# Refitting a list scheduler's cost model to the trace: engine latencies, transfer time and table loads in a one-core attention-and-MLP kernel

## Chip, core and metric

The kernel runs on one core of a Trainium2 chip. The metric is device time in microseconds (us) of one execution. Medians over several executions are quoted with their range. All runs quoted are in the undisturbed state, at a granted clock of 0.992 or more, except one execution that is named where it occurs. All kernels here give a correct result.

## The reference

`x` is 2048 x 1024, the MLP's inner width is 3584, all in bf16. Cut to what matters:

```python
def reference(A_x, A_wqkv, A_wo, B_x, B_w_gate, B_w_up, B_w_down):
    def _A_ref(x, wqkv, wo):                       # linear attention, 32 heads of 32
        ...                                        # q, k, v = split(x @ wqkv)
        phi = lambda t: jnp.where(t > 0, t + 1, jnp.exp(t)) + 1e-6
        pq, pk = phi(q), phi(k)
        kv = jnp.einsum("bhsd,bhse->bhde", pk, v)
        ...                                        # o = (pq @ kv) / (pq . z)
        return (lambda x, *d: x.transpose(*d))(o, 0, 2, 1, 3).reshape(B, S, D) @ wo
    def _B_ref(x, w_gate, w_up, w_down):
        g = _silu(x @ w_gate)
        u = x @ w_up
        return (g * u) @ w_down
    x = A_x
    xn = _layernorm(x, axis=-1)
    s = _A_ref(xn, A_wqkv, A_wo)
    g = _silu(_B_ref(xn, B_w_gate, B_w_up, B_w_down))
    return x + s * g
```

## The kernel before

The kernel is a program that plans itself on the host. Each piece of work (a group of matmuls, an activation, a VectorE operation, a transfer) becomes an `Op` with an engine, an assumed duration and the data that it reads and writes. `Plan.schedule` plays the program through with these assumed times, and the order in which operations start in that play becomes the order of each engine's queue. `emit` then puts semaphore waits between them. The assumed times never change what is computed. They change above all who stands behind whom in each queue. One thing more hangs on the engine latencies: a load may not be issued before the group of TensorE's work that lies 12 us ahead of its deadline, and the deadlines count these latencies. Run again on the host, the plan after lets 134 of its 257 transfers go later than the plan before, by a median of 1.7 us of TensorE's work; the transfer model, the PE to PE rule and the table part leave these gates where they were.

```python
class Plan:
    ENGS = ("pe", "act", "dve", "pool", "sp")
    LAT = {"pe": 0.25, "act": 0.3, "dve": 0.3, "pool": 0.3}      # from end of work to "others may start"
    ...
    def schedule(self):
        ...                                                       # deadlines o.dl, backwards from TensorE's order
        while len(order) < total:
            best = None
            for e in self.ENGS:
                ...
                if e == "pe":
                    ...                                           # a window of 6 groups
                    rdy = [o for o in cand if o.ready <= t + 0.05]
                    o = min(rdy, key=lambda o: o.idx) if rdy else min(cand, key=lambda o: (o.ready, o.idx))
                else:
                    rdy = [o for o in a if o.ready <= t]
                    o = min(rdy, key=lambda o: (o.dl - o.boost, o.idx)) if rdy else min(a, key=lambda o: (o.ready, o.dl))
                s = max(t, o.ready)
                if best is None or s < best[0]:
                    best = (s, e, o)
            s, e, o = best
            o.start = s
            if o.sem is not None:                                 # a transfer, issued by SyncE
                free[e] = s + 0.08
                b = max(s + 1.0, dma_free)
                dma_free = b + o.nbytes / 230e3
                o.done = dma_free + 1.8
            else:
                free[e] = s + o.busy
                o.done = s + o.busy + o.lat
            ...
            for q in o.succs:
                q.npred -= 1
                q.ready = max(q.ready, o.done)
                if q.npred == 0:
                    avail[q.eng].append(q)
```

The picker for VectorE and ScalarE takes, among the operations that it believes ready, the one with the earliest deadline.

Why TensorE cares about VectorE's order: the large products are done with Strassen-like sets of seven half-size products, and the sums between them are made in PSUM. In a set, ScalarE copies the first product to a second bank, and VectorE adds a stored product to a bank; the next matmuls go on top of that bank.

```python
            def put1(self, a):
                self.a = a
                self.b = balloc()
                act([bank_r[a]], [bank_r[self.b]], ps[self.b][:, :], ps[a][:, :], ACT.Identity)
            ...
                elif m == 6:
                    self.grp(6, self.b, False)
                    self.c = balloc()
                    tt([bank_r[self.b], self.s5.r], [bank_r[self.c]], ps[self.c][:, :], ps[self.b][:, :],
                       self.s5.ap(F32), ALU.add)                  # VectorE: "ps<-ps,TM" in the trace
                ...
                elif m == 3:
                    self.grp(3, self.c, False)                    # TensorE needs that bank
```

The same VectorE queue also takes operations on data that has just been loaded: the layer-norm statistics of each row tile of `x` (`stats<-W`), the sums of weight blocks (`W<-W`, `W<-X`, from `w_gate`, `w_up`, `w_down`), and the last multiply and add of each output tile on transposed data (`TM<-TM`). `x` tiles in the attention part come so:

```python
        def x_load(i):
            s = x_ring.take()
            xslot[i] = s
            dma([], [s.r], s.ap(), xf[i * 128:(i + 1) * 128, :], dsem("x%d" % s.k), 256 * KB).urgent = 10.0

        def ln_tile(i):
            ...
            o0 = dve([s.r], [sA], lambda h: h.bn_stats(stats[:, j, 0, :], xa[:, 0:512]), 512)
            ...
```

## Time and profile before

| kernel before | value |
|---|---|
| median of 3 executions | 731.58 us (731.02 to 731.81) |
| profiled span | 729.5 us |
| TensorE / VectorE / ScalarE busy | 715.9 / 612.8 / 400.5 us |
| table loads on ScalarE | 10, 1.28 us each |

TensorE is busy for 98% of the span, so the reader should look not at shares of busy time but for the few places where TensorE pauses. Two rulers are used. The first is the table of busy time by stretch. The second, finer one is worked out from the trace: the time from one matmul's start to the next, less its columns over 2.4 GHz, counted where more than 40 ns remain. I call these pauses.

One view of the kernel before is not in the prediction, and it turned out to be the one that mattered: the list of what each engine waited for. The columns are engine, what it was about to write, the line of the program, the releaser, then us in total, number of waits and the longest of them.

```profile
DVE W L348 <- DMA W<-in_B_w_down_dram: 7.0, 2, 3.6
DVE TM L348 <- DMA TM<-TM: 3.4, 5, 1.3
DVE stats L649 <- DMA W<-in_A_x_dram: 2.5, 2, 2.4
...
PE ps L210 <- DVE ps L348: 1.4, 5, 0.4
```

Before the change VectorE stood idle ahead of a transfer ten times, 13.2 us in all; TensorE waited for VectorE's additions in PSUM for 1.4 us.

### The profile page before, as it was taken

To read this page: it belongs to the slowest core of one execution; us is meant where nothing else is said; L and a number is where in the kernel's file an instruction comes from. 1 tells how busy PE (TensorE), PEld (TensorE's weight loads), DVE (VectorE), ACT (ScalarE), POOL (GpSimd) and SP (SyncE) were. 2 spreads that over 40 slices of the span, in tenths; PEclk is the share of its full clock that TensorE was granted. 3 is DMA by queue.
4 is the path that set the end of the run, shared out by engine and by line. 5 is a ranking of instruction groups with operands and counts; after the bars stand their busy time and mean duration, and the time that the engine had idled before them with its cause. 6 is when DMAs were issued, how large, how long until landed. Compare 5 with 4: busy or idle time off the path is not lost.

```text
span 729.5 us, 10728 instructions
## 1 busy us (share of the span) xinstructions
PE 715.9 (98%) x3942; PEld 371.1 (51%) x3942; DVE 612.8 (84%) x1443; ACT 400.5 (55%) x759; POOL 14.1 (2%) x35
## 2 busy tenths in 40 slices
PE   8999999999999999999999999999999999999996
PEld 3444444455555555554444445555555555544442
DVE  6999868979989998898555989999999888865662
ACT  3776654787659665654111177676966756511111
POOL 2111000000000000000000000000000000000000
PEclk9999999999999999999999999999999999999999
DMA  8443235135255343324279554134515343546633
GB/s 291 113 104 85 44 107 181 59 107 168 73 159 139 129 143 129 94 73 132 79 186 245 145 165 149 62 116 120 172 59 188 102 130 118 143 123 181 164 89 87
DMA packets 135668, 94.02 MB, mean 129 GB/s; under 512 B 32960, under 2 KB 131520, under 8 KB 135616
## 3 DMA queue, kind: packets, MB, share of 16 engines
q1 hardware_dynamic: 135616, 93.34, 44.9%
q8 instruction: 31, 0.51, 0.3%
q14 instruction: 21, 0.17, 0.1%
HBM read 75.50 MB, written 10.62 MB: 118 GB/s over the span
## 4 chain that ended last, share of the span: by engine, by line
PE 85%; ACT 7%; DVE 5%; issue 2%; POOL 0%; ACTq 0%; DVEq 0%; POOLq 0%
PE ps L210 85%; ACT H L341 3%; ACT TM L341 2%; DVE W L348 2%; DVE H L348 1%; DVE TM L348 1%; ACT ps L341 1%; DVE ps L348 1%; ACT L341 1%; DVE stats L649 0%; DVE stats L653 0%; DVE TM L724 0%; PE ps L217 0%; DVE X L348 0%; POOL rstd L658 0%
## 5 line engine op out<-in xcount | busy, mean ns | idle before, releaser
L210 PE MATMUL ps<-X,W 128*128 128x512 f16 (+1 forms) x1232 | 268.0, 358 | 1.1 <-ACT ps L341 0.5
L341 ACT ACTIVATE TM<-ps 128x512 f16<-128x512 f32 (+2 forms) x345 | 184.2, 553 | 147.8 <-PE ps L210 143.9
L210 PE MATMUL ps<-H,W 128*128 128x512 f16 (+2 forms) x1168 | 256.4, 369 | 0.5 <-DVE ps L348 0.5
L348 DVE TENSOR_TENSOR W<-W 128x256 f16<-128x256 f16 (+5 forms) x440 | 176.4, 437 | 7.2 <-DMA W<-in_B_w_down_dram 7.0
L210 PEld LDWEIGHTS ps<-H,W 128*128 128x128 f16 (+1 forms) x1168 | 113.5, 98 | 124.1 <-DVE ps L348 2.3
L210 PEld LDWEIGHTS ps<-X,W 128*128 128x128 f16 (+1 forms) x1232 | 119.3, 98 | 102.8 <-ACT ps L341 2.2
L348 DVE TENSOR_TENSOR ps<-ps,TM 128x256 f32<-128x256 f32 (+1 forms) x234 | 123.5, 531 | 15.0 <-PE ps L210 14.0
L341 ACT ACTIVATE ps<-ps 128x512 f32<-128x512 f32 (+1 forms) x164 | 81.9, 499 | 72.2 <-PE ps L210 70.1
L210 PE MATMUL ps<-P,W 128*128 128x512 f16 (+1 forms) x496 | 104.7, 329 | 0.7 <-ACT TM L341 0.4
L341 ACT ACTIVATE H<-ps 128x512 f16<-128x512 f32 (+1 forms) x126 | 75.0, 602 | 54.5 <-PE ps L210 54.2
L210 PEld LDWEIGHTS ps<-P,W 128*128 128x128 f16 (+1 forms) x496 | 48.3, 98 | 37.9 <-ACT ps L341 1.0
L348 DVE TENSOR_TENSOR H<-H 128x1024 f16<-128x1024 f16 (+4 forms) x106 | 66.1, 640 | 1.0 <-ACT H L341 0.5
L348 DVE TENSOR_TENSOR TM<-ps,TM 128x512 f32<-128x512 f32 (+1 forms) x60 | 40.7, 678 | 24.0 <-PE ps L210 23.7
L210 PE MATMUL ps<-W 128*128 128x256 f16 (+1 forms) x278 | 56.5, 289 | 0.6 <-DVE ps L348 0.4
L348 DVE TENSOR_TENSOR H<-H,TM 128x512 f16<-128x512 f16 x112 | 44.8, 415 | 14.0 <-ACT H L341 13.8
L341 ACT ACTIVATE TM<-TM 128x512 f16<-128x512 f32 (+1 forms) x61 | 37.9, 624 | 33.4 <-DVE TM L348 32.5
L210 PEld LDWEIGHTS ps<-W 128*128 128x128 f16 (+1 forms) x278 | 26.1, 98 | 21.3 <-DVE ps L348 2.3
L210 PE MATMUL ps<-H,X 128*128 128x512 bf16 (+1 forms) x136 | 32.2, 379 | 1.2 <-ACT X L341 0.8
L210 PE MATMUL ps<-TM,W 128*128 128x256 f16 (+1 forms) x138 | 27.8, 283 | 0.3 <-DVE ps L348 0.3
L348 DVE TENSOR_TENSOR P<-H 128x1024 f16<-128x1024 f16 x28 | 19.0, 686 | 9.2 <-PE ps L210 9.2
L723 DVE TENSOR_SCALAR TM<-TM 128x512 f16<-128x512 f16 x64 | 17.7, 285 | 10.5 <-ACT TM L341 10.3
L348 DVE TENSOR_TENSOR H<-ps,TM 128x512 f16<-128x512 f32 (+1 forms) x35 | 23.9, 682 | 2.3 <-PE ps L210 1.7
(81 smaller groups left out, 394.9 us busy)
## 6 DMA issues: line engine op xcount, KB each, us to landing
W<-in_B_w_down_dram SPq DMA_DIRECT2D x16, 896.0 KB, 5.8
W<-in_B_w_gate_dram SPq DMA_DIRECT2D x12, 1024.0 KB, 5.4
W<-in_B_w_up_dram SPq DMA_DIRECT2D x12, 1024.0 KB, 5.5
W<-in_A_x_dram SPq DMA_DIRECT2D x16, 256.0 KB, 3.0
H<-in_A_wqkv_dram SPq DMA_DIRECT2D x8, 512.0 KB, 8.2
H<-r_scratch SPq DMA_DIRECT2D x32, 128.0 KB, 3.4
W<-m_scratch SPq DMA_DIRECT2D x4, 1024.0 KB, 5.9
s_scratch<-TM SPq DMA_DIRECT2D x32, 128.0 KB, 2.8
```

The lines of the kernel that those rows point to most:

```text
L210: last = h.matmul(o, l, r, start=st, stop=sp, skip_group_check=True)
L341: return PL.op("act", reads, writes, lambda h: h.activation(o, i, func, **kw), nel(o) / 1200.0 + (0.055 if src == "ps" else 0.095))
L348: return dve(reads, writes, lambda h: h.tensor_tensor(o, a, b, op), nel(o), 1.92 if fast else 0.96)
L723: dve([e.r], [b.r], lambda h: h.tensor_scalar(ba, ea, 1.0, EPS_PHI, ALU.min, ALU.add), 512, 2.6)
```

## The change

The intent: make the scheduler's assumed times those which the trace shows, and let it know that ScalarE loads a table when it changes between Exp and Silu. The core of the diff (the `Op` slot, the reset of `tab` and context lines are cut):

```diff
-    LAT = {"pe": 0.25, "act": 0.3, "dve": 0.3, "pool": 0.3}
+    LAT = {"pe": 0.2, "act": 0.165, "dve": 0.14, "pool": 0.15}
...
+                if e == "act" and o.tab is not None and o.tab != tab:
+                    s += TABLE                                   # 1.28
...
+            if o.tab is not None:
+                tab = o.tab
...
-                b = max(s + 1.0, dma_free)
-                dma_free = b + o.nbytes / 230e3
-                o.done = dma_free + 1.8
+                b = max(s + 1.1, dma_free)
+                dma_free = b + o.nbytes / 330e3
+                o.done = dma_free + 1.0
...
-                q.ready = max(q.ready, o.done)
+                q.ready = max(q.ready, o.done if q.eng != "pe" or o.eng != "pe" else s + o.busy)
...
         def act(reads, writes, o, i, func, src="ps", **kw):
-            return PL.op("act", ..., nel(o) / 1200.0 + (0.055 if src == "ps" else 0.095))
+            q = PL.op("act", ..., nel(o) / (1000.0 if "bias" in kw or not isinstance(kw.get("scale", 1.0), float)
+                      else 1200.0) + (0.055 if src == "ps" else 0.095))
+            q.tab = func if func != ACT.Identity else None
+            return q
```

Four parts: engine latencies (LAT), no latency from TensorE to TensorE (PE to PE), the transfer model (DMA), and tables with the slower ScalarE rate.

More of the change, by code (lines that the diff above doesn't have):

```diff
@@ L16 @@
 GRAN = 256
+TABLE = 1.28
 class Op:
     __slots__ = ("eng", "fn", "busy", "lat", "nbytes", "sem", "preds", "succs", "idx", "dl", "start", "done",
-                 "ev", "pecum", "npred", "ready", "urgent", "boost")
+                 "ev", "pecum", "npred", "ready", "urgent", "boost", "tab")
 class Region:
@@ L52, in op @@
         o.boost = 0.0
+        o.tab = None
         o.idx = len(self.ops)
@@ L108, in schedule @@
         dma_free = 0.0
+        tab = None
         avail = {e: [] for e in self.ENGS}
@@ L340, in act @@
         def act(reads, writes, o, i, func, src="ps", **kw):
-            return PL.op("act", reads, writes, lambda h: h.activation(o, i, func, **kw),
-                         nel(o) / 1200.0 + (0.055 if src == "ps" else 0.095))
+            q = PL.op("act", reads, writes, lambda h: h.activation(o, i, func, **kw),
+                      nel(o) / (1000.0 if "bias" in kw or not isinstance(kw.get("scale", 1.0), float) else 1200.0)
+                      + (0.055 if src == "ps" else 0.095))
+            q.tab = func if func != ACT.Identity else None
+            return q
         def dve(reads, writes, fn, n, rate=0.96):
```

## The prediction

> **What bounds the kernel now.** I read the busy line first, then a table of engine busy time by stretch, then TensorE's order of time around each hole in that table.
>
> The engine line and the granted clock, from the page of the kernel before:
>
> ```profile
> PE 715.9 (98%) x3942; PEld 371.1 (51%) x3942; DVE 612.8 (84%) x1443; ACT 400.5 (55%) x759; POOL 14.1 (2%) x35
> PEclk9999999999999999999999999999999999999999
> ```
>
> TensorE is busy 98% of a 729.5 us span at full clock. Only 729.5 - 715.9 = 13.6 us are idle. The change alters no matmul, so it can work only on that idle time and on the short pauses inside "busy". Where are they? Engine busy time by stretch (us from the start; each entry is busy time and number of instructions):
>
> ```profile
> 0.00:8.00 8.00, 6.38 (x22) 2.39 (x22) 3.93 (x11) 1.66 (x2) 4.05 (x21) 1.00 0.61 205
> 8.00:32.00 24.00, 22.24 (x121) 10.13 (x122) 21.79 (x46) 14.18 (x20) 3.42 (x4) 1.00 0.61 196
> 32.00:120.00 88.00, 88.00 (x495) 43.51 (x494) 73.71 (x176) 53.80 (x87) 6.61 (x10) 1.00 0.41 106
> 120.00:140.00 20.00, 18.22 (x105) 9.15 (x103) 19.62 (x63) 13.82 (x26) 0.00 (x0) 1.00 0.35 115
> 220.00:245.00 25.00, 24.17 (x138) 12.77 (x136) 24.24 (x61) 23.59 (x47) 0.00 (x0) 1.00 0.48 130
> 720.00:729.50 9.50, 3.57 (x19) 1.49 (x17) 2.05 (x5) 1.19 (x2) 0.00 (x0) 0.87 0.43 99
> ```
>
> TensorE's column is the third figure. Idle: 1.6 us before 8 us, 1.8 up to 32 us, 1.8 in 120 to 140, 0.8 in 220 to 245, 5.9 after 720; what is left (13.6 - 11.9 = 1.7) lies in 400 to 437 and 465 to 531. All else is full. A stall also hides some 0.16 us in "busy", because a matmul is recorded as 379 ns long while the next can start after 216. So I also summed start-to-start times less columns/2.4 GHz from the trace's matmul starts, counting only excesses over 40 ns. Three heaps come out: 2.7 us in the 14 cold matmuls at the head; 3.3 us of waits between 7.6 and 31.8 us; 8.3 us between 117 and 568 us (2.5 at 134 to 139, 1.6 at 229 to 244, 1.6 at 416 to 436, 1.0 at 466 to 491, 1.0 at 518 to 530, the rest 0.1 or less each). After the last of the big groups comes the tail.
>
> The largest hole, in order of time on ScalarE and TensorE:
>
> ```profile
> 134.78 1.57 ACT L341 ACTIVATE TM<-ps 128x512 f16<-128x512 f32 x3
> 136.37 1.28 ACT L341 ACT_TABLE_LOAD   x1
> 137.66 0.60 ACT L341 ACTIVATE TM<-ps 128x512 f16<-128x512 f32 x1
> 138.31 0.88 PE L210 MATMUL ps<-H 128*128 128x512 bf16 x3 [1.27 <-ACT TM L341]
> ```
>
> TensorE waits 1.27 us for a PSUM bank that ScalarE empties only after a table load. The tail, after the last down-projection matmuls:
>
> ```profile
> 720.42 2.75 PE L210 MATMUL ps<-P,W 128*128 128x512 f16 x12
> 723.21 0.60 ACT L341 ACTIVATE TM<-ps 128x512 f16<-128x512 f32 x1 [1.99 <-PE ps L210]
> 724.65 0.94 SPq L351 DMA_DIRECT2D out_dram<-TM  x2
> ```
>
> From 723.17 to 729.5 is Silu, multiply, four transposes, add and the store: 6.3 us of one dependent chain.
>
> **What the Trainium skill says.** "TensorE: Matmul & The Clock Gate", on the cold and warm issue gap, gives N/1.2 GHz cold and N/2.4 GHz plus about 2.5 ns warm: 427 and 216 ns at N = 512. The trace agrees: 428 ns for the warm-up matmuls, 216 ns for 2669 others. The floor follows: all matmul columns over 2.4 GHz are 702.1 us, plus 3942 x 2.6 ns = 10.2, gives 712.4 us. "ScalarE: Activation LUTs", What ACT_TABLE_LOAD costs, says about 1283 ns for the load and 1380 ns of drain with it. The ten loads here have the first figure exactly (12.8 us for 10) but no such drain: the Silu above starts 1.29 us after the load starts. So the change's constant of 1.28 is the right one here.
>
> **The change part by part.** Nothing is removed from or added to the work: same matmuls (2726 of 512 columns, 1044 of 256), same rings, same buffers. Only the constants by which the program builder orders each engine's queue are altered.
>
> (1) Engine latencies: 0.25 for TensorE and 0.3 for the others become 0.2, 0.165, 0.14, 0.15. The trace backs them. A 512-wide activation lasts 0.60 us, its hand-over shows as 0.05 of issue, and the scheduler counts 0.482 of it as busy: 0.60 + 0.05 - 0.482 = 0.17. VectorE: 0.69 + 0.05 - 0.603 = 0.14. TensorE: 0.379 + 0.05 - 0.216 = 0.21.
>
> (2) TensorE after TensorE now has no latency. Before, the next group on the same bank looked 0.25 us late, past the tolerance of 0.05, so the scheduler put in another group. The orders show it: TensorE's listing falls from 889 to 775 rows, its semaphore waits from 625 to 563, and the down projection runs 84 matmuls of one kind, then 14, where before they alternated 7 and 2. Matmuls cost 216 ns either way, so this alone buys nothing.
>
> (3) DMA: 1 MB was modelled as 1.0 + 4.56 + 1.8 = 7.4 us, now 1.1 + 3.18 + 1.0 = 5.3; the trace has 5.4 for w_gate. Loads are not waited for by TensorE anywhere in the middle, so no gain; at the head see below.
>
> (4) ScalarE with a bias or scale pointer: 1024-wide from 0.948 to 1.12 us (trace: 1.15 start to start, 29.27 to 30.42), 512-wide from 0.52 to 0.61 (trace about 0.64). This should help the 16 scaled copies in 220 to 245, where ScalarE is busy 23.6 of 25 us.
>
> (5) Tables: the delay is added to the start of the operation that has already been picked by deadline; it does not make the picker prefer the loaded table. I counted loads in both compiled orders: 10 and 10. The three in quick succession at 423 to 431 us are still three, two or fewer activations apart. "Keeps apart" saves 0 x 1.28 us. What remains is that other engines are planned around a busy ScalarE.
>
> The sum. Middle: a planner whose constants match the trace should avoid perhaps 45% of stalls that arise because its plan is wrong; the rest come from ScalarE or VectorE being full (24.2 of 25 us on VectorE in 220 to 245). This 45% is my judgement: 0.45 x 8.3 = -3.7 us.
> Head: worked through by hand with the times of before. The weight blocks landed at 6.8, 8.6, 10.1 and 11.65 us. The new TensorE order takes 16 matmuls on all four blocks before the second tile's transposes, where before it took 4. From 8.27 us: block three is wanted at 10.0, waits 0.15; block four is wanted at 11.0, waits 0.65; the transposes run 12.53 to 12.98; their eviction (1.02 us, behind an Exp) ends about 14.2, so a third wait of 1.3. That is 2.1 us of new waits against 0.3 removed (the one at 15.4). By 24.3 us the new order should be at its fourth transposes with 8 matmuls (1.7 us) fewer behind it, but without the 0.4 us wait at 19.8 and 0.6 at 24.4. Some of the later 1.3 us (26 to 31.8) should go too. Net +0.4 us.
> Tail: the same chain after the same last matmul, 0.
> Total -3.7 + 0.4 = -3.3 us: 731.6 - 3.3 = 728.3, say 728.2.
>
> **The rivals.** A: the stalls nearly all go. For it: every constant now fits the trace. Against: at 229 to 238 both helpers are full, and a table load of 1.28 us in front of a bank that is needed costs the same however well it is known. Bound: 8.3 + 3.3 = 11.6 us, so 720 at the very best.
> B: the old, too long latencies were a margin; a fitted order breaks on what is still not modelled (each DMA issue is counted as 0.08 us but four took 2.15 us; the cold 14 matmuls are counted at 216 ns). For it: the head, where I find new waits for weight blocks because the plan now expects them too early. Against: in the middle TensorE waited for no DMA. It would give 732 to 735.
> C: nothing visible, because stalls just move to other places under ScalarE's load bursts. 730 to 732. The same ten table loads speak for it.
>
> **Range and chances.** Two per cent is 14.6 us. The bound of A is 11.6, so faster by 2% is out of reach: 0.01. Slower by 2% would need an in-order queue blocked for 15 us: 0.02. Between A and B I take 728.2, with 723.5 to 732.5 for 8 in 10.
>
> **What would show it.** Right: ten loads of 1283 ns again; matmul starts 216 ns apart; a new TensorE wait near 11 us and one near 13 us for ScalarE's X; TensorE idle in 120 to 531 us falling from 5.1 to about 3; a tail of about 6.3 us. Wrong: idle in the middle as before or larger (C or B); new waits on DMA in the middle; a tail longer by a microsecond, because queue order at the end differs; or a head that gives back several microseconds.

## The result

The change made the kernel **slower by 0.9%**: 737.45 us median of four executions (736.41 to 739.13) against 731.3 us for the kernel before in the same rounds (731.02 to 731.81). The ratio is 1.0086, with a 95% interval of 1.0064 to 1.0107. Ratios here and below are the mean time of one kernel's fast runs over the mean of the other's in the same rounds, so they are not quite the ratios of the medians quoted. The prediction was 728.2 us with 723.5 to 732.5 as range: it expected a gain of 3.3 us, and there is a loss of 6.2 us. The class within 2% was right, the direction and the range were wrong. All outputs are right.

The profiled execution of the kernel after is the slowest of the four (739.13 us, span 737.4 us), so the traces differ by 7.9 us where the medians differ by 6.2. Its page:

```profile
span 737.4 us, 10770 instructions
...
PE 716.1 (97%) x3942; PEld 371.4 (50%) x3942; DVE 611.7 (83%) x1443; ACT 399.8 (54%) x759; POOL 16.3 (2%) x35
```

Every engine does the same work in the same time: TensorE 716.1 us against 715.9, ScalarE 399.8 against 400.5, VectorE 611.7 against 612.8. All of the difference, by this account, is idle time of TensorE (slow matmuls count as busy: 1.7 us more of them at 51 us and 1.3 us less in the warm-up, see below, nearly cancel). The table loads, from the groups of instructions by shape (busy time, mean ns of one, idle before):

```profile
L350 ACT ACT_TABLE_LOAD x10 | 12.8, 1283 | 1.0 <-PEq L1449 0.8
```

Ten, as before: nothing was kept apart. Where the idle time is shows in the table by stretch (TensorE's is the third figure; number of instructions in brackets). After:

```profile
32.00:120.00 88.00, 86.02 (x468) 42.12 (x466) 73.27 (x175) 51.57 (x82) 7.78 (x10) 0.98 0.38 85
120.00:140.00 20.00, 20.00 (x125) 10.96 (x122) 17.49 (x50) 11.77 (x22) 0.00 (x0) 1.00 0.46 148
220.00:245.00 25.00, 22.05 (x128) 11.99 (x126) 22.99 (x60) 22.06 (x44) 0.00 (x0) 1.00 0.56 154
531.00:720.00 189.00, 187.06 (x989) 95.60 (x987) 150.00 (x334) 84.75 (x170) 0.00 (x0) 1.00 0.47 134
```

The last stretch before the change, which the prediction did not show:

```profile
531.00:720.00 189.00, 189.00 (x998) 97.23 (x996) 146.64 (x326) 80.78 (x162) 0.00 (x0) 1.00 0.45 128
```

The hole at 134 to 139 us, the prediction's chief example, has left its stretch: TensorE is busy for all 20 us, where it had been busy for 18.2. It has not gone, though. It lies just past the stretch's end, at 139.6 to 141.5 us, and is half as large (1.2 us of pauses, by the finer ruler, where there were 2.5). TensorE waits there for the same operation behind the same table load:

```profile
139.06 1.28 ACT L350 ACT_TABLE_LOAD   x1
...
141.00 0.61 PE L219 MATMUL ps<-H 128*128 128x512 bf16 x2 [0.99 <-ACT TM L350]
```

And there are new holes: 2.0 us between 32 and 120 us (with a granted clock of 0.98, the one stretch between warm-up and tail under 1.00), 3.0 instead of 0.8 us at 220 to 245 us, and 1.9 instead of 0 us between 531 and 720 us. The pauses of both traces, summed from the matmuls' starts, by place:

| pauses of TensorE, us | before | after | difference |
|---|---|---|---|
| cold matmuls of the warm-up | 2.7 | 1.4 | -1.3 |
| head, to 31.8 us | 3.3 | 4.7 | +1.4 |
| 49 to 55 us | 0 | 3.9 | +3.9 |
| middle, 117 to 645 us | 8.3 | 12.3 | +4.0 |
| tail after the last group of matmuls | 6.3 | 6.3 | 0 |

The differences sum to 8.0 us, the spans differ by 7.9. In the middle the larger items are -1.3 (134 to 142 us), +1.8 (222 to 244), +1.6 (397 to 417), -0.7 (420 to 437), +1.2 (561 to 575) and +1.1 (644).

Now the same list of waits as above, after the change:

```profile
DVE TM L360 <- DMA TM<-TM: 24.2, 10, 5.7
...
DVE W L360 <- DMA W<-in_B_w_down_dram: 10.0, 5, 2.3
DVE stats L661 <- DMA W<-in_A_x_dram: 6.9, 3, 2.5
...
PE ps L219 <- DVE ps L360: 4.7, 6, 1.2
...
PE ps L219 <- DVE TM L736: 2.0, 1, 2.0
DVE W L360 <- DMA W<-m_scratch: 1.4, 1, 1.4
DVE W L360 <- DMA X<-in_B_w_gate_dram: 1.2, 1, 1.2
```

VectorE now stands idle ahead of transfers 27 times, 47.6 us in all (13.2 before), and TensorE waits for VectorE's work on PSUM 4.7 + 2.0 us where it was 1.4. The two belong together. VectorE's own order of time around the hole at 49 us (start, duration, and in brackets the idle time before with its releaser):

```profile
45.75 0.68 DVE L665 BATCH_NORM_STATS2 stats<-W 128x6 f32<-128x512 bf16 x1
48.92 0.69 DVE L661 BATCH_NORM_STATS2 stats<-W 128x6 f32<-128x512 bf16 x1 [2.49 <-DMA W<-in_A_x_dram]
...
50.60 0.68 DVE L736 SCALAR_TENSOR_TENSOR TM<-ps,TM 128x512 bf16<-128x512 f32 x1
```

TensorE in the same time:

```profile
48.33 1.03 PE L219 MATMUL ps<-H,W 128*128 128x512 f16 x4
51.34 1.20 PE L219 MATMUL ps<-H,X 128*128 128x512 bf16 x4 [1.98 <-DVE TM L736]
...
53.20 3.89 PE L219 MATMUL ps<-H,W 128*128 128x512 f16 x12
```

And TensorE there before the change:

```profile
48.27 1.03 PE L210 MATMUL ps<-H,W 128*128 128x512 f16 x4
49.13 0.63 PE L210 MATMUL ps<-H,TM 128*128 128x129 bf16 x8
...
50.46 2.75 PE L210 MATMUL ps<-H,W 128*128 128x512 f16 x12
```

What is to be seen: the statistics of an `x` tile stand at the head of VectorE's queue, and the tile has not landed. VectorE stands still for 2.49 us. Behind it in the queue is the operation of line 736, which reads a PSUM bank and so frees it for TensorE. It could have run. Pairing the plan, run again on the host, with the trace shows that its bank had been full since 46.8 us, and that all else it needed was a short VectorE operation (0.29 us) in the same queue, whose data was there at 47.5 us. VectorE was idle, but the queue is in order. TensorE waits 1.98 us (2.15 from start to start). And the damage goes on: twelve matmuls then take 3.89 us where twelve of the same shape took 2.75, because TensorE's clock fell to half rate after the hole. Over 16 matmuls, eight of them only 129 columns wide, that is 1.7 us more. The stretch of the fall (the clock is the figure 0.50):

```profile
52.08:55.49 3.41, 3.41 (x16) 1.79 (x15) 2.01 (x7) 0.58 (x1) 0.00 (x0) 0.50 0.61 151
```

At 235 us the load is another one, `m_scratch`, but the pattern is the same; in order of time:

```profile
233.74 0.89 DVE L360 TENSOR_TENSOR W<-W 128x256 f16<-128x256 f16 x2 [1.38 <-DMA W<-m_scratch]
...
235.15 0.42 DVE L360 TENSOR_TENSOR ps<-ps,TM 128x256 f32<-128x256 f32 x1
...
235.63 0.39 PE L219 MATMUL ps<-W 128*128 128x256 f16 x2 [1.13 <-DVE ps L360]
```

At 562 us it is a block of `w_gate`: 1.24 us of VectorE idle, then an addition in PSUM, then TensorE after 0.89 us of waiting. At 397 us VectorE stands 5.7 us ahead of a transposed output tile.

Followed back operation by operation in the same way, TensorE's pauses at 49, 235, 242, 397, 407, 562 and 644 us all lead to such a stop of VectorE: 8.6 us, or 10.3 with the half-rate matmuls. Three more (222, 520 and 524 us, 1.8 us) lead to ScalarE, which stands ahead of a load from `r_scratch`. In the kernel before, no wait of TensorE over 0.2 us leads to a transfer. The sum is more than the 7.9 us lost, because other pauses of the kernel before went away.

**How early is the new plan?** The planned time from issue to landing on an idle queue is 2.8 us + bytes / 230 GB/s in the old model and 2.1 us + bytes / 330 GB/s in the new; measured is the median from issue to landing in the transfer view.

| transfer | old plan | new plan | measured before / after |
|---|---|---|---|
| `x` tile, 256 KB | 3.9 | 2.9 | 3.0 / 2.9 |
| `x` tile for the output, 256 KB | 3.9 | 2.9 | 4.4 / 4.6 |
| `w_down` block, 896 KB | 6.8 | 4.9 | 5.8 / 6.0 |
| `w_up` block, 1 MB | 7.4 | 5.3 | 5.5 / 5.4 |
| transpose of an output tile | 3.7 | 2.7 | 2.4 / 2.8 |

The new plan sits at the median of some transfers and well under that of others. The old plan was over the median of four of the five. The tile at 49 us was issued at 43.32 us and landed 5.6 us later, at 48.90; the plan, run again on the host, has 4.1 us for it (2.9, and a wait for the transpose ahead of it). SyncE also spent 1.24 us on issuing that transpose and 0.58 us on the tile, and the plan counts 0.08 us for each. So the transfer itself was 1.5 us slower than planned, and its issue came 1.2 us later after the transpose's; together that is about the 2.49 us for which VectorE stood.

### The profile page after: what moved, and what is told of

It is laid out like the page before. It is cut to its first block, busy times and chain, and to the rows that moved or that the text cites. A ratio compares the mean times of both kernels' runs of the same rounds, so it can differ in the third digit from the quotient of the medians.

```text
span 737.4 us, 10770 instructions
## 1 busy us (share of the span) xinstructions
PE 716.1 (97%) x3942; PEld 371.4 (50%) x3942; DVE 611.7 (83%) x1443; ACT 399.8 (54%) x759; POOL 16.3 (2%) x35
## 4 chain that ended last, share of the span: by engine, by line
PE 81%; DMA 9%; DVE 6%; ACT 2%; SPq 1%; issue 1%; POOL 0%; ACTq 0%
PE ps L219 81%; DMA W<-in_A_x_dram 2%; DVE W L360 2%; DVE H L360 2%; DMA W<-in_B_w_up_dram 2%; DMA X<-in_B_w_gate_dram 1%; DMA W<-m_scratch 1%; DMA W<-in_B_w_down_dram 1%; DMA H<-r_scratch 1%; DMA X<-in_A_wqkv_dram 1%; ACT TM L350 1%; SPq L363 1%; DVE ps L360 1%; DVE TM L360 1%; DMA X<-s_scratch 0%
## 5 line engine op out<-in xcount | busy, mean ns | idle before, releaser
L219 PE MATMUL ps<-H,W 128*128 128x512 f16 (+2 forms) x1168 | 252.1, 370 | 2.0 <-DVE ps L360 2.0
L219 PE MATMUL ps<-P,W 128*128 128x512 f16 (+1 forms) x496 | 99.5, 329 | 0.0
L360 DVE TENSOR_TENSOR TM<-ps,TM 128x512 f32<-128x512 f32 (+1 forms) x60 | 40.7, 679 | 11.7 <-PE ps L219 11.3
L360 DVE TENSOR_TENSOR TM<-TM 128x512 bf16<-128x512 f16 (+1 forms) x29 | 12.2, 419 | 24.2 <-DMA TM<-TM 24.2
L219 PE MATMUL ps<-H,P 128*128 128x512 bf16 (+1 forms) x96 | 23.5, 379 | 0.0
```

The lines of the kernel that those rows point to most:

```text
L219: last = h.matmul(o, l, r, start=st, stop=sp, skip_group_check=True)
L360: return dve(reads, writes, lambda h: h.tensor_tensor(o, a, b, op), nel(o), 1.92 if fast else 0.96)
```

## Experiments

**Theory D** (formed from the traces above): the new transfer model expects transfers too early. VectorE's queue then has an operation on a load at its head that cannot start yet, with work on PSUM behind it that TensorE needs. **Rival L**: the loss is of the fitted engine latencies, whose old, too long values were a margin. **Rival R**: any change of the order costs some us, because the order before happened to be a good one. **Rival Q**: the plan is early because it counts 0.08 us for an issue by SyncE which takes 0.3 to 1.2 us.

### Parts of the change, one by one

`dma_back`: the kernel after with the old transfer model.

```diff
-                b = max(s + 1.1, dma_free)
-                dma_free = b + o.nbytes / 330e3
-                o.done = dma_free + 1.0
+                b = max(s + 1.0, dma_free)
+                dma_free = b + o.nbytes / 230e3
+                o.done = dma_free + 1.8
```

> The changed kernel with the three DMA constants put back (230 instead of 330 per us, fixed parts 1.0 and 1.8); all else new. Theory D (the new DMA constants make VectorE queue work that waits for a transfer ahead of PSUM additions that TensorE needs): the loss goes, 726 to 732 us, and VectorE's idle time before transfers falls from about 48 us to 15 or less. Theory L (the fitted engine latencies took away a margin): still 735 or more, idle before transfers no matter. Theory R (any other constants reshuffle the list by several us either way): anything in 728 to 738.

Measured: 732.13 us (731.86 to 732.64), ratio to the kernel before 1.0008 [0.9993, 1.0023]. VectorE's idle time ahead of transfers is 14.7 us. Taking back the transfer model alone takes away the loss (0.6 us of it may be left), so without that part there is hardly any. The later gates of the loads, which this version keeps, are not the cause then.

`dma_only`: the kernel before with nothing but the new transfer model (the same lines the other way round).

> The kernel before with only the three DMA constants changed. Theory D: 735 to 740 us, VectorE idle before transfers 35 us or more, as in the changed kernel. Theory L: 730 to 732, as before. Theory R: anything in 728 to 738, with no tie to the idle time before transfers.

Measured: 743.23 us (741.9 to 744.58), ratio 1.0159 [1.0144, 1.0174]. It alone does more harm than the whole change; which of the other parts softens it, and how, was not traced. VectorE idles 38.5 us ahead of transfers, and the pattern is at its plainest here. The order of time near the end:

```profile
704.29 0.63 DVE L348 TENSOR_TENSOR W<-W 128x896 f16<-128x896 bf16 x1 [6.08 <-DMA W<-in_B_w_down_dram]
...
706.57 0.68 DVE L348 TENSOR_TENSOR TM<-ps,TM 128x512 f32<-128x512 f32 x1
...
707.31 0.60 PE L210 MATMUL ps<-P,W 128*128 128x512 f16 x2 [2.29 <-DVE TM L348]
```

VectorE stands for 6.08 us before a `w_down` block; the operation on PSUM that frees a bank starts 2.3 us after it gets going again; TensorE has waited 2.29 us. Here too the clock then falls to half rate:

```profile
708.51:711.92 3.41, 3.41 (x10) 1.22 (x8) 3.08 (x7) 0.60 (x1) 0.00 (x0) 0.50 0.45 115
```

`lat_pe_only`: the kernel before with the new LAT and the PE to PE rule.

```diff
-    LAT = {"pe": 0.25, "act": 0.3, "dve": 0.3, "pool": 0.3}
+    LAT = {"pe": 0.2, "act": 0.165, "dve": 0.14, "pool": 0.15}
...
-                q.ready = max(q.ready, o.done)
+                q.ready = max(q.ready, o.done if q.eng != "pe" or o.eng != "pe" else s + o.busy)
```

> The kernel before with only the engine latencies and the rule for TensorE after TensorE changed; DMA, ScalarE rate and tables as before. Theory D: 727 to 732 us, my prediction's middle gain of 3.7 us would show here. Theory L: 734 or more. TensorE's order should have the long runs (84 and 14) of the changed kernel in either case.

Measured: 734.09 us (733.78 to 735.26), ratio 1.0037 [1.0022, 1.0052]. The fitted latencies cost 2.6 us on their own, with VectorE's waits for transfers as they were (14.7 us). About 2.2 us of it lies in one place: three table loads in quick succession at 428, 430 and 432 us, after which TensorE waits up to 1.6 us for a PSUM addition behind ScalarE's late result. So rival L is real, though smaller than D.

`lat_only` and `pp_only`: each half of that alone, the first two or the last two changed lines of the diff just shown.

> The kernel before with the four fitted engine latencies alone. My prediction's middle gain should stand here if anywhere: 727 to 729. If instead the old latencies were a harmless or useful margin: 731 to 734, carrying the 2.6 us loss of the joint run.

> The kernel before with only the rule for TensorE after TensorE. Theory: groups on one bank now run in one piece, matmuls keep their 216 ns: 731 to 732. If the interleaving of before hid VectorE's and ScalarE's hand-overs: 733 to 735, the 2.6 us loss of the joint run.

Measured: LAT alone 735.49 us (735.28 to 735.54), ratio 1.0053 [1.0036, 1.007]; PE to PE alone 735.77 us (735.63 to 737.79), ratio 1.0064 [1.0049, 1.0079]. Each alone costs about 4 us, both together 2.6, and both with the table and rate part 0.6 (that is `dma_back`). These effects do not add. A change of any of these constants reorders the queues and can open or close holes of 1 to 2 us anywhere. Why each half alone is worse than both together was not traced further and stays open. Two things should be known: LAT also moves the gates of the loads, and its share of the cost was not separated; and the profiled execution of `pp_only` is the slowest of its four (737.79 us), with a stretch of 3.41 us at half clock from 27.89 us on.

`tab_act_only`: the kernel before with the table term and the slower ScalarE rate alone.

```diff
+                if e == "act" and o.tab is not None and o.tab != tab:
+                    s += TABLE
...
-                         nel(o) / 1200.0 + (0.055 if src == "ps" else 0.095))
+                      nel(o) / (1000.0 if "bias" in kw or not isinstance(kw.get("scale", 1.0), float) else 1200.0)
+                      + (0.055 if src == "ps" else 0.095))
```

> The kernel before with only the table term and the ScalarE rate with pointer operands. Ten table loads in any case. Theories D and L: 729 to 732 us, near the kernel before; more than 734 would speak for R.

Measured: 731.27 us, ratio 0.9995 [0.9979, 1.0012], VectorE's idle time 13.5 us. Nothing gained, nothing lost.

### Is it VectorE's queue?

`dve_slack`: the kernel after, whose plan adds 2.0 us to the landing of a transfer, but only as seen by VectorE's operations.

```diff
                 q.ready = max(q.ready, o.done if q.eng != "pe" or o.eng != "pe" else s + o.busy)
+                if o.sem is not None and q.eng == "dve":
+                    q.ready = max(q.ready, o.done + 2.0)
```

`other_slack` is the control: the same margin for all but VectorE.

```diff
+                if o.sem is not None and q.eng != "dve":
+                    q.ready = max(q.ready, o.done + 2.0)
```

> The changed kernel, but in the plan a transfer's data count as ready 2.0 us later for VectorE's operations alone (nothing is waited for longer on the chip; only the order changes). Theory D (head-of-queue blocking of VectorE): 728 to 733 us, VectorE idle before transfers from 48 to 18 us or less. If lateness hurts through another engine: 736 or more.

> The control: the same 2.0 us for every consumer of a transfer except VectorE. Theory D: stays at 735 to 741 us, VectorE idle before transfers still above 35 us. If the optimism hurts through other engines, or any later estimate helps: 728 to 733.

Measured: the margin for VectorE gives 731.45 us, ratio 0.9997 [0.9982, 1.0012]; the same margin for everyone else gives 740.59 us (738.1 to 740.68), ratio 1.0111 [1.0092, 1.013]. VectorE's idle time ahead of transfers is 22.7 us in the first and 52.3 us in the second. This separates D from the rest: to undo the loss, nothing of the new transfer model has to be taken back except what VectorE's queue is told about it. By medians the control was slower still than the kernel after, which is more than D says, but their ranges overlap.

What `dve_slack` still lacked shows in its trace at 506 us: two scaled activations on ScalarE start after 2.13 us of idle ahead of a load from `r_scratch`, a PSUM copy for TensorE stands behind them, and TensorE waits 1.66 us. It is the same pattern in ScalarE's queue.

`x_slack`: the same margin only for the later `x` tiles, the loads behind the hole at 49 us.

```diff
+                if o.sem is not None and o.urgent == 10.0:
+                    q.ready = max(q.ready, o.done + 2.0)
```

> The changed kernel with 2.0 us of planned slack for the later loads of x alone, the transfers behind the 2.1 us hole at 49 us. Theory D, read at one place: the hole goes and with it the 16 matmuls at half rate after it, so TensorE's progress curve at 57 us of the kernel before is 3 us or more nearer to before, and the later holes (234, 243, 407, 561, 644 us) stay: 733 to 735 us. If the half-rate matmuls come from something else than the hole, they stay: 735 or more.

Measured: 734.43 us (732.67 to 736.0), ratio 1.004 [1.0021, 1.0058]; 3.0 us better than the kernel after, where the hole and its cold matmuls had been 3.9. TensorE at the place:

```profile
48.39 1.03 PE L221 MATMUL ps<-H,W 128*128 128x512 f16 x4
...
50.59 2.75 PE L221 MATMUL ps<-H,W 128*128 128x512 f16 x12
```

No wait, and twelve matmuls in 2.75 us again. VectorE's total idle time ahead of transfers is still 46.4 us here, against 47.6: **that total is not a measure of the loss**. It costs only where TensorE's work on PSUM stands behind it.

### Rivals R and Q

`before_nudge`: the kernel before with 232 GB/s in place of 230, a change without meaning that still reshuffles.

```diff
-                dma_free = b + o.nbytes / 230e3
+                dma_free = b + o.nbytes / 232e3
```

> The kernel before with 232 for 230 in the transfer rate, a change without meaning. Theory R (any change of constants reshuffles by several us): off by 2 us or more. Theory D: 730.5 to 732.5.

Measured: 731.82 us, ratio 1.0003 [0.9988, 1.0017]. Together with `tab_act_only` it speaks against R in its strong form: the order before is not so lucky that every change costs. That `lat_only` and `pp_only` cost 4 us each says that the weak form holds: several us hang on the order.

`sp_real`: the kernel after, which plans SyncE's issues at 0.5 us, and the transposes at 1.3 us.

```diff
-                free[e] = s + 0.08
+                free[e] = s + (1.3 if o.nbytes in (200 * KB, 400 * KB) else 0.5)
```

> The changed kernel, with the issue queue's own time per transfer planned as the trace has it (0.5 us, 1.3 for a transposing transfer) instead of 0.08. If the transfers come later than planned because their issue is late behind transposes (sub-theory Q): 729 to 734 us, and the 2.1 us hole at 49 us gone. If they come late because the transfer itself is slower than planned (sub-theory T): 735 or more.

Measured: 735.88 us (733.97 to 737.72), ratio 1.0057 [1.0037, 1.0077]; VectorE's idle time is 41.9 us. By medians 1.6 of some 6 us come back, and the ranges overlap. A hole remains at the same place: TensorE waits 1.48 us there instead of 1.98. Q is a part at most. At this place 1.2 of some 2.7 us of the earliness were in the issue time (above), so more than half was not.

### How much margin?

`all_slack`, `slack1`, `slack4`: the kernel after with 2.0, 1.0 and 4.0 us for every consumer of a transfer.

```diff
+                if o.sem is not None:
+                    q.ready = max(q.ready, o.done + 2.0)      # 1.0, 4.0
```

> The changed kernel with 2.0 us of slack in the plan for every consumer of a transfer (sum of the two slack runs). Theory D extended to any in-order queue: the 1.8 us hole at 506 us that ScalarE's wait for the reciprocals makes in the run with VectorE's slack alone goes: 728.5 to 731 us. If slack for VectorE alone is all that counts: 731 to 732, and the hole stays.

> Dose: 1.0 us of slack for every consumer (0 gave 737.5, 2.0 gave 728.8). Theory D: between, 730 to 735, VectorE idle before transfers between 24 and 48 us. If the 2.0 result was a lucky order: anything, 736 or more included.

> Dose: 4.0 us. Theory D: no better than 2.0, since by then no planned operation overtakes its transfer: 727 to 732, VectorE idle before transfers 20 us or less; a larger slack can cost something where work is queued later than its data come. If the 2.0 result was lucky: 734 or more.

Measured: 2.0 us gives 728.84 us (727.24 to 729.64), ratio 0.996 [0.9945, 0.9975], the first version that is faster than the kernel before. 1.0 us gives 731.4 us (730.03 to 732.99), ratio 1.0 [0.9982, 1.0017]. 4.0 us gives 744.23 us (743.91 to 744.75), ratio 1.0177 [1.016, 1.0194]: a clear miss, since I had expected it near the others. Its VectorE waits for transfers are the least of all with the new model (10.9 us), but another queue is now in the way. ScalarE and TensorE in order of time:

```profile
443.04 0.75 ACT L352 ACTIVATE ps<-ps 128x256 f32<-128x256 f32 x2
...
443.47 0.61 PE L221 MATMUL ps<-W 128*128 128x256 f16 x2 [5.33 <-ACT ps L352]
```

TensorE waits 5.33 us, more than in any other hole that this document shows, for a PSUM copy that stands in ScalarE's queue behind a table load, a wait for a store (0.25 us) and one for VectorE (1.69 us). The clock is at half rate for 3.41 us afterwards. Holes of 2.0 us at 236 and of 1.3 us at 272 and 580 us add to it. A margin that is too large makes the plan put work behind loads too late, and the order then fails elsewhere. Which operation's lateness begins this chain was not settled.

`all_slack_oldlat`: 2.0 us for all, with the old LAT and without the PE to PE rule.

```diff
-    LAT = {"pe": 0.2, "act": 0.165, "dve": 0.14, "pool": 0.15}
+    LAT = {"pe": 0.25, "act": 0.3, "dve": 0.3, "pool": 0.3}
...
-                q.ready = max(q.ready, o.done if q.eng != "pe" or o.eng != "pe" else s + o.busy)
+                q.ready = max(q.ready, o.done)
+                if o.sem is not None:
+                    q.ready = max(q.ready, o.done + 2.0)
```

> The same slack, with the old engine latencies and the old rule for TensorE after TensorE. If the fitted latencies cost time by themselves (the run with them alone was 2.6 us slower): 1 to 3 us faster than the slack run with fitted latencies, 727 to 730. If they are neutral once transfers have slack: within 1 us of it.

Measured: 729.9 us (728.76 to 730.33), ratio 0.9975 [0.996, 0.999]. The fitted latencies are worth at most 1 us on top of the margin, and the ranges overlap. That they cost 2.6 us with the old transfer model and cost nothing here shows that L is no rule about latencies.

### The version that beats both

`slack2_head`: 2.0 us for all, and the 14 warm-up matmuls planned at 0.4 us, as the trace has them, instead of 0.216. `slack18_head` and `slack23_head`: the same with 1.8 and 2.3 us, to see whether 2.0 is luck.

```diff
-            pe_mm([ident_r, wz_r], [bank_r[b]], [(ps[b][:, :], ident[:, :], wz, True, True)])
+            PL.op("pe", [ident_r, wz_r], [bank_r[b]],
+                  partial(_mm_group, [(ps[b][:, :], ident[:, :], wz, True, True)]), 0.4)
```

> The slack of 2.0 with the 14 warm-up matmuls planned at 0.4 us instead of 0.216, as the trace has them while the clock is cold. The order at the head still takes 16 matmuls on four weight blocks first, so I expect little: 727 to 730. If the head's 1 to 2.6 us loss of the slack run comes from TensorE being planned too early, 726 to 728.

> Slack of 1.8 us instead of 2.0, warm-up planned at 0.4 us: is the best version a lucky order? If the gain of 2.8 us belongs to the constants, 727.5 to 730.5. If it is luck, 731 to 737, the spread of the single-part runs.

> The same with 2.3 us. Belongs to the constants: 727.5 to 730.5. Luck: 731 to 737. The run with 4.0 us lost 12.8 us, so a beginning of that loss, 731 to 733, would show a narrow best.

Measured: 2.0 us gives 728.66 us (728.28 to 729.44), ratio 0.9963 [0.9948, 0.9978]; 1.8 us gives 728.98 us (728.25 to 729.2 in its three fast executions), ratio 0.9962 [0.9945, 0.9979]; 2.3 us gives 728.82 us (728.43 to 728.95), ratio 0.996 [0.9944, 0.9977]. One of the four executions at 1.8 us, the profiled one, took 1268.22 us at a granted clock of 0.557; it is left out as a slow run, and no reading rests on its trace. The three neighbours agree within 0.4 us, so the gain of 2.7 us over the kernel before is not one lucky order. The warm-up's planned time adds nothing that shows (728.66 against 728.84).

All runs together, with VectorE's idle time ahead of transfers from each profile:

| run | median us | ratio to before | VectorE idle ahead of transfers, us |
|---|---|---|---|
| kernel before | 731.3 | 1 | 13.2 |
| kernel after | 737.45 | 1.0086 | 47.6 |
| dma_back | 732.13 | 1.0008 | 14.7 |
| dma_only | 743.23 | 1.0159 | 38.5 |
| lat_pe_only | 734.09 | 1.0037 | 14.7 |
| lat_only | 735.49 | 1.0053 | 6.7 |
| pp_only | 735.77 | 1.0064 | 14.8 |
| tab_act_only | 731.27 | 0.9995 | 13.5 |
| dve_slack | 731.45 | 0.9997 | 22.7 |
| other_slack | 740.59 | 1.0111 | 52.3 |
| x_slack | 734.43 | 1.004 | 46.4 |
| before_nudge | 731.82 | 1.0003 | 14.2 |
| sp_real | 735.88 | 1.0057 | 41.9 |
| slack1 | 731.4 | 1.0 | 25.4 |
| all_slack | 728.84 | 0.996 | 23.0 |
| all_slack_oldlat | 729.9 | 0.9975 | 14.5 |
| slack4 | 744.23 | 1.0177 | 10.9 |
| slack2_head | 728.66 | 0.9963 | 21.4 |
| slack18_head | 728.98 (fast runs) | 0.9962 | not read |
| slack23_head | 728.82 | 0.996 | not read |

## Why the prediction was wrong, and where it was right

**The step that failed is item (3), the transfers.** It reads: "Loads are not waited for by TensorE anywhere in the middle, so no gain". The premise was true, and the conclusion asked the wrong question. It took "TensorE waits for no load" to mean "when loads are expected does not matter", and looked neither at VectorE's queue nor at what stands behind a load in it. The list of waits of the kernel before already had VectorE waiting 7.0 us for `w_down`, 3.4 for transposes and 2.5 for `x`: a sign that its order is set close to the landings. One fact that the step needed is in the Trainium skill, "TensorE: Matmul & The Clock Gate", the specification table at its head: VectorE's queue is strictly first in, first out, while TensorE's can pull weight loads ahead. The trace agrees: VectorE idle for 2.49 us at 49 us with runnable PSUM work behind it. What the runs showed in its place: the new transfer model alone costs 11.7 us (`dma_only`), without it the loss is 0.6 us at most (`dma_back`), and with 2 us of margin for VectorE's queue alone it is gone (`dve_slack`, 731.45 us), while the same margin for everyone else leaves it (`other_slack`, 740.59 us). VectorE's waits for transfers rose from 13.2 to 47.6 us, and TensorE's pauses behind them are the 8.6 us found above (10.3 with the half-rate matmuls). This is the main cause.

**The sum's first term, -3.7 us for the middle, had the wrong sign.** It was a judgement that a plan closer to the trace loses fewer stalls. Measured: +4.0 us in the middle and +3.9 us at 49 to 55 us, a place where the prediction saw no stall at all. The hole that carried the argument, at 134 us, lost half of its 2.5 us (-1.3 us); the 1.2 us that stayed stand behind the same table load, as the prediction's case against rival A has it (a known table load costs the same). At 420 to 437 us 0.7 us went too. These gains were outweighed. What the judgement missed is that an estimate's errors do not weigh the same on both sides. An estimate at the median is too early in half of the cases. In an in-order queue, being early blocks everything behind, and being a little late costs little while there is other work (how much is too late, `slack4` shows). The old model's 7.4 us for a transfer of 5.4 was a margin; the new model with 2.0 us added plans 7.3 us for it, and is again on the good side.

**Rival B named the mechanism and was set aside for the same reason.** "Against: in the middle TensorE waited for no DMA." It also named what was not modelled (the issues, the cold matmuls); these turned out to be a part at most: `sp_real` returned 1.6 us by medians, the warm-up nothing that shows. Its 732 to 735 us was too mild, too: it measured 737.45.

**The head was right in its waits.** Predicted new waits of 0.15, 0.65 and 1.3 us; measured 0.150, 0.617 and 1.324 us. Predicted net +0.4 us; at 37 us, when TensorE had done 30 us of work, the kernel after was about 0.1 us behind. The pauses of the head are 1.4 us more and those of the warm-up 1.3 less. The latter is a matter of the run: 12 cold matmuls in the trace of before, 7 in that of after, with the same 14 issued. And most of the former is its other side: after the quicker warm-up TensorE stood for 1.2 us until the first tile was ready, and its first transposes began at 7.01 us where they had begun at 7.19.

**Tables and tail were right.** Ten loads of 1283 ns, none saved; 6.3 us of tail in both.

**(2), PE to PE, "alone buys nothing", was too kind:** alone it costs 4 us (`pp_only`), as LAT does (`lat_only`). So a part of what rival B said about latencies holds, but only in some combinations.

**Two readings of the pauses were slightly off.** The prediction has 1.0 us at 466 to 491 and 1.0 at 518 to 530 us; the trace gives 0.8 and 1.1. Their sum of 8.3 us stands.

**The check that I set myself had a wrong starting figure.** I wrote of idle "falling from 5.1 to about 3" in 120 to 531 us. The table by stretch has 411.0 - 406.75 = 4.25 us before, and 411.0 - 404.65 = 6.35 after, so it rose. In `slack2_head` it is 411.0 - 408.0 = 3.0, with nothing idle between 32 and 120 us. The gain that the prediction gave to the change, to 728.2 us, is what the change with a margin reaches (728.7 us). That both numbers come from the same holes was not tested one by one.

## What to carry to other kernels

When a host-side plan sets the order of in-order queues, give it transfer times that are rarely exceeded, not median ones, and put the margin where the consumer's queue also carries work that the bounding engine needs; here 2 us on a transfer of 3 to 6 us was worth 8.6 us against none, while 4 us cost more than none. Before changing such a model, read what *every* engine waits for and what stands behind each of those waits, not only what the bounding engine waits for. And test the parts of a refit singly: of four parts that all fit the trace better, one cost 12 us alone, two cost 4 us each, and one did nothing.

## What the Trainium skill lacked or had wrong

- "TensorE: Matmul & The Clock Gate", Part 1: The HAM clock gate, says that the clock falls to half rate after at least one idle window of about 3.4 us. Here TensorE did not have to be idle for so long. In the kernel after it was still busy for 1.43 of the 3.41 us before the fall at 52.08 us, in `dma_only` for 1.20 us before the fall at 708.51 us. In `pp_only` two pauses of 1.1 and 0.9 us, with 1.69 us of work in 3.41, came before the fall at 27.89 us. A pause of 2.0 us at 464 us in `other_slack` was followed by no fall, so the length of one pause does not decide it. Each of these stretches at half rate lasted 3.41 us. That the number of cold matmuls at the start varies from run to run, as the page says, agrees: 12 and 7.
- "ScalarE: Activation LUTs", What ACT_TABLE_LOAD costs: the load of 1283 ns is exact, but of the drain of 1380 ns that the page adds there is nothing here; in both kernels the next activation starts 1.29 us after the load starts, in eight of the nine loads after the first (the ninth then waits for TensorE).
- "DMA: Bandwidth & Descriptors" has cycle counts for issuing a transfer in generations before trn3, but no page has the time that it costs in a run like this. In the kernel after SyncE was occupied for 0.30 to 0.58 us by nine copies in ten and for about 1.2 us by most transposes (up to 2.2), and once for 4.14 us by a single copy of 256 KB (392 us).
- The strict order of VectorE's queue is stated (on the page of TensorE, and not only there); no page has its consequence for planning, that one operation put ahead of its transfer holds up unrelated PSUM work: 27 such waits with 47.6 us in all, and behind them 8.6 us of pauses of TensorE (10.3 with the half-rate matmuls).
